# Threshold attention followed by a token and channel mixer: merged transfers, later planned places for VectorE behind transfers, and all of x turned by block transposes

## The chip, the cores and the metric

The kernel runs on one core of one Trainium2 chip. The metric is device time in microseconds (us), lower is better: the median of several runs. The engines are TensorE (PE in the profile, with its weight loads as PEld), VectorE (DVE), ScalarE (ACT), GpSimd (POOL) and SyncE (SP), which here only issues transfers (DMA). Each engine runs its instructions in program order.

## The reference

Eight batches b, eight heads, sequence S = 576, head size 64. Attention keeps only scores within tau of the row's maximum; its output is then x of a mixer block of width 512.

```python
scores = scale * np.matmul(q, k.transpose(0, 1, 3, 2))
thresh = np.max(scores, axis=-1, keepdims=True) - tau
scores = np.where(scores >= thresh, scores, -1000000000.0)
scores = scores - np.max(scores, axis=-1, keepdims=True)
attn = np.exp(scores)
attn = attn / (np.sum(attn, axis=-1, keepdims=True) + 1e-09)
attn_out = np.matmul(attn, v)
x = attn_out.transpose(0, 2, 1, 3).reshape(B, S, H * D)
xt = x.transpose(0, 2, 1)
h = np.maximum(xt @ w_tok1, 0.0) @ w_tok2
u = x + h.transpose(0, 2, 1)
h2 = np.maximum(u @ w_ch1, 0.0) @ w_ch2
return u + h2
```

All arrays are float32 (weights arrive as 64-bit words and are converted in the kernel).

## The kernel before

**Attention.** Heads are taken in pairs (four pairs per batch), and two pairs make a quad of 9 units of 128 query rows, so a batch has 18 units. A round is two units: scores on PE (L825) into the one pair of score tiles, row maxima on DVE (`mx`, L842), the bias on POOL (L848), the mask on ACT (L858), the exponentials on ACT (L868), the inverse sums on DVE (L276, L277), the scaling on POOL (L285). From batch 1 on, the scaled unit `e` is turned in 32x32 blocks on DVE (`turn_blocks`, L315, into a tile `T`), and four transfers per unit (`move`, L327) bring the blocks to the right partitions of `eT`. Three units make a group; a group's values (V: L365 and L370) give a part of x, already transposed, as `xT` (copied by ACT or DVE at L374). So a batch has two quads of three groups. Batch 0 turns `e` on PE (L300) instead.

**Token mixing.** Its first layer needs x with tokens on the partitions, in `x_sb`. In batch 0, PE transposes turn all of x (L435, copied out at L439). From batch 1 on, the first quad's half is turned early, while the second quad is still in attention (`early_x`): two DVE block transposes into the tile `extra` (L395), four transfers to `x_sb` (L406), one small DVE transpose (L401) and four small transfers (L412). The second quad's half is turned by ten PE transposes (L435) after its last V. Then come the first layer on PE (L454), relu, the second layer (L472) and the addition to `xT` on DVE (L483), which makes u.

**Channel mixing.** Groups of 256 rows of u: first layer L948, relu on ACT or DVE (L953, L956), second layer L964. Batch 0 does two such groups at once, batches 1 to 6 one each. For batches from 1 on, u itself is turned back by DVE (L933, into `us`) and transfers (L940, from `us` to `ut`), added to the second layer's result by DVE (L978, into `us`), and stored (L988). `us` has one buffer, so the next L933 waits for these stores. All the rest of u is spilled (L531) and done at the end, from about 904 us on, by another scheme (lines above 1200), which the change leaves alone.

**What sets the order.** The program is written by a planner (class `Scheduler`, L568 on): each operation has an engine, a cost, dependences and a rank (lower goes first); the planner simulates the engines' clocks and eight transfers in flight, and writes each engine's instructions in the order in which it would start them. A dependence on a transfer counts from its planned landing. The score rounds of the next batch are held back by a plan (`planned_at`) so that some channel work of the batch before is left when a batch's attention ends (the planner's constants KEEP and KEEP_LAST, 14 and 20). All transfers in the middle go through SP's one queue, where an instruction that waits holds back all behind it.

**Conversion.** Thirty-one pieces of weights are loaded (L200) into three raw buffers in turn and converted by ACT, DVE and POOL (L239, the last step); the third raw buffer is the place of the last two weight pieces themselves, so the last but one piece has a buffer `spare_a` of its own.

Of the kernel before, what the change touches and what calls it, by code (L numbers as in the profile page):

```python
# [21 lines left out]
def kernel(  # L22
# [166 lines left out]
    def load_piece(i):  # L189
# [7 lines left out]
        if i == len(pieces) - 2:  # L197
            raw_at[i % NRAW] = att.tile([P, 2 * WMAX], U32, tag="spare", bufs=1, name="spare_a")
        raw = raw_at[i % NRAW][0:rows, 0 : n * (2 if wide(i) else 1)].bitcast(src.dtype)
# [110 lines left out]
    def turn_blocks(u):  # L310

        b, p0, t = units[u]
        e = st.pop(u)
        T = Ts[u] = att.tile([P, 4, NK * 32], F32, tag="T", bufs=3, name=f"T_{u}")
        nc.vector.transpose(  # L315
            out=T.rearrange("p a (c x) -> p c a x", c=NK), in_=e.rearrange("p (c a x) -> p c a x", c=NK, a=4)
        )

    def move(u):
        b, p0, t = units[u]  # L320
        key, place = (b, p0, t // GU), t % GU
        if place == 0:
            turned_e[key] = att.tile([P, GU, 4, NK * 32], F32, tag="eT", name=f"eT_{u}")
            eTs[key] = turned_e[key].rearrange("p n i (c x) -> p (n i) c x", c=NK)
        T = Ts.pop(u)
        for i in range(4):
            nc.sync.dma_start(  # L327
                out=turned_e[key][:, place, i, :], in_=T[32 * i : 32 * i + 32]
            )
# [56 lines left out]
    HQ = NP // 2  # L386

    def early_x(b):
# [5 lines left out]
        def turn_main(c):  # L394
            nc.vector.transpose(  # L395
                out=main[:, :, :, c, :].rearrange("q a t d -> q t a d"),
                in_=xT[:, c, 0:MAIN].rearrange("q (t r a) -> q t a r", t=NI, a=4),
            )

        def turn_rest():  # L400
            nc.vector.transpose(  # L401
                out=rest.rearrange("q a c d -> q c a d"), in_=xT[:, 0:HQ, MAIN:S].rearrange("q c (r a) -> q c a r", a=2)
            )

        def move_main(i):
            nc.sync.dma_start(  # L406
                out=x_sb[:, 0:NI, 32 * HQ * i : 32 * HQ * i + 32 * HQ],
# [3 lines left out]
        def move_rest(i):  # L411
            nc.sync.dma_start(  # L412
                out=x_sb[0:LAST, NI, 32 * HQ * i : 32 * HQ * i + 32 * HQ],
# [5 lines left out]
    def token_mlp(b, ps=range(NP)):  # L419
# [4 lines left out]
        turned = ps[HQ:] if b else ps  # L424
# [18 lines left out]
        def tok1(bank, m):  # L443
            if b not in hidden:
                hidden[b] = work.tile([P, NTK, DM], F32, tag="a", bufs=1, name=f"a_{b}")
            if K == L:
                products = [(cols, lambda t: x_sb[:, t, cols])]
            else:
# [37 lines left out]
        for t, n in [(t, n) for t in range(0, NI, n)] + [(NI, 1)]:  # L486
# [62 lines left out]
    FLIGHT, RATE, LANDING = 8, 214.0, 1.5  # L549
# [18 lines left out]
    class Scheduler:  # L568
# [35 lines left out]
        def start(self, x, eng):  # L604
            t = max([d.landed or d.end + (d.lag if d.eng != eng else 0.0) for d in x.deps] + [0.0])
# [113 lines left out]
    CONV = len(pieces)  # L719
    CR = (1, 1, 2)  # L720
# [26 lines left out]
    def make_conversion():  # L747
        for part in range(2):
            put_ac(0, part)
        for i in range(CONV):  # L750
# [5 lines left out]
            put_load(i + NRAW, (key_op("pool", i),))  # L756
# [18 lines left out]
    def make_pair(n):  # L775
# [32 lines left out]
        put(("split", n), sched.op("dve" if n >= NP else "pool", 0.25 if n >= NP else 0.5, lambda: split_middle(n), (key_op("loadv", n), free), 2))  # L808
# [97 lines left out]
    def make_early(b):  # L906

        turn_main, turn_rest, move_main, move_rest = early_x(b)
        have = [key_op("X", rank_of_group(b, 0, g)) for g in range(3)]
        free = early.get(b - 1, converted)  # L910
        turns = [sched.op("dve", 1.1, lambda c=c: turn_main(c), have + free, 2) for c in range(HQ)]
        before = [x for k, x in keyed.items() if k[0] == "tok" and k[1] == b - 1 and len(k) == 3 and x.first_layer]
        moved = [sched.op("sp", 1.2, lambda i=i: move_main(i), turns + before, 0, dmas=(1, 131, 0.645)) for i in range(4)]
        last = sched.op("dve", 0.35, turn_rest, moved, 2)
        moved += [sched.op("sp", 0.6, lambda i=i: move_rest(i), [last] + before, 0, dmas=(1, 16, 0.6)) for i in range(4)]
        early[b] = moved
        xreads.setdefault(b, []).extend(turns + [last])

    def make_groups(b, halves):
        uT = xTs[b]  # L920
        reads = []
        for i in range(NOW[b]):
# [3 lines left out]
            def new_us(s=s, i=i):  # L926
                s["us"] = work.tile([P, nt, 4, NCC * 32], F32, tag="us", bufs=1, name=f"us_{b}_{i}")

            def turn_u(s=s, i=i):
                new_us(s)  # L930
                s["ut"] = work.tile([P, nt, 4, NCC * 32], F32, tag="ut", bufs=1, name=f"ut_{b}_{i}")
                for m in range(nt):
                    nc.vector.transpose(  # L933
                        out=s["us"][:, m].rearrange("q a (c d) -> q c a d", c=NCC),
# [3 lines left out]
            def move_u(k, s=s):  # L938
                for m in range(nt):
                    nc.sync.dma_start(  # L940
# [547 lines left out]
```

## Time and profile before

| what | value |
|---|---|
| time, median of 3 runs | 1267.58 us (1266.56 to 1271.94) |
| the profiled execution: time | 1273.39 us |
| the profiled execution: span of its instructions | 1271.4 us |
| mean granted clock of TensorE | 0.991 |
| 504 transfers eT<-T (L327), 144 KB each | 3.0 us from issue to landing |
| 28 transfers x_sb<-extra (L406), 128 KB each | 3.2 us |
| 28 transfers x_sb<-extra (L412), 16 KB each | 1.9 us |
| 128 transfers ut<-us, 64 KB each | 2.1 us |
| 126 block transposes T<-e on DVE (L315) | 1362 ns each, 170.0 us |
| 14 block transposes extra<-xT on DVE (L395) | 1112 ns each, 15.3 us |
| 12 block transposes us<-xT on DVE (L933) | 1088 ns each, 12.6 us |
| 90 transposes of x on PE (L435) | 10.9 + 3.5 us busy |

The span runs from the first instruction's start to the last one's end. Busy times of an engine can be added up and set against the span; where two instructions of PE overlap in its pipeline, the sum of their own times is more than the room that they take. The granted clock is the share of full speed that TensorE was given. A wait is idle time of an engine, put down to the instruction that released it last.

### The profile page before, as it was taken

The page shows a single profiled execution, that of the slowest core. Times are in us where ns is not written, and L with a number is a line of the kernel's source. Part 1 is how long each engine was busy: PE and PEld are TensorE (multiplying, and loading weights), DVE is VectorE, ACT ScalarE, POOL GpSimd, SP SyncE. Part 2 cuts the span into 40 slices and gives each one's busy share as a digit, 9 for nine tenths or more (in the row PEclk, how much of TensorE's full clock was granted, in tenths as well). Part 3 has the DMA queues.
Part 4 walks back from the last instruction along what each step waited for, and adds up shares of the span by engine and source line. Part 5 has one row for each costly group of instructions (what it writes and reads, how often), then busy time and mean ns, then how long its engine had stood idle before and what let it go on. Part 6 is the DMA issues. An engine that isn't in the chain of part 4 may idle for free.

```text
span 1271.4 us, 21773 instructions
## 1 busy us (share of the span) xinstructions
PE 1237.8 (97%) x8150; PEld 1015.3 (80%) x8150; DVE 755.0 (59%) x1163; ACT 564.0 (44%) x1233; POOL 315.4 (25%) x518
## 2 busy tenths in 40 slices
PE   8888999999999999999989999999999999999998
PEld 7656778797678778878867777888988888888887
DVE  6699982656666667756666756761443534444443
ACT  6998862554645545556465455531110202011120
POOL 4565641232223333323323322410001010000100
PEclk9899999999999999999999999999999999999999
DMA  9546985366777786786776875750212101021011
GB/s 167 139 124 166 214 212 131 87 128 160 168 164 175 160 169 150 165 178 137 179 148 135 187 159 111 179 150 1 60 23 67 34 25 42 18 67 25 26 34 33
DMA packets 324216, 149.23 MB, mean 117 GB/s; under 512 B 223696, under 2 KB 316880, under 8 KB 324112
## 3 DMA queue, kind: packets, MB, share of 16 engines
q1 hardware_dynamic: 322240, 147.64, 50.5%
q8 instruction: 64, 1.05, 0.4%
q10 hardware_dynamic: 1872, 0.21, 0.1%
q14 instruction: 40, 0.33, 0.1%
HBM read 47.32 MB, written 13.50 MB: 48 GB/s over the span
## 4 chain that ended last, share of the span: by engine, by line
PE 78%; SPq 6%; DVE 5%; DMA 5%; ACT 4%; issue 2%; POOL 0%; DVEq 0%; ACTq 0%; POOLq 0%
PE bank L964 11%; PE bank L948 10%; PE o L1309 10%; PE sc L825 9%; PE bank L370 7%; PE hx L1309 6%; PE bank L454 5%; PE hmm L1309 4%; PE oz L1309 4%; PE hz L1309 4%; PE bank L472 4%; SPq L327 3%; PE bank L365 2%; DVE mx L842 2%; ACT e L858 2%
## 5 line engine op out<-in xcount | busy, mean ns | idle before, releaser
L285 POOL TENSOR_SCALAR e<-e,rr 128x576 f32<-128x576 f32 x288 | 213.2, 758 | 299.1 <-DVE rr L277 286.6
L858 ACT ACTIVATE e<-sc,bias 128x576 f32<-128x576 f32 x288 | 194.1, 740 | 156.8 <-POOL bias L848 155.1
L842 DVE TENSOR_REDUCE mx<-sc 128x2 f32<-128x1152 f32 x144 | 188.1, 1347 | 58.9 <-PE sc L825 58.4
L868 ACT ACTIVATE e<-e,ntau 128x576 f32<-128x576 f32 x288 | 220.4, 778 | 0.3
L315 DVE STREAM_TRANSPOSE T<-e 128x1152 f32<-128x1152 f32 x126 | 170.0, 1362 | 36.1 <-POOL e L285 22.2
L948 PE MATMUL bank<-xT,wc 128*128 128x256 f32 x768 | 181.0, 389 | 6.1 <-ACT g L953 5.1
L964 PEld LDWEIGHTS bank<-wc,g 128*128 128x128 f32 x1536 | 178.0, 192 | 10.4 <-issue 2.4
L964 PE MATMUL bank<-wc,g 128*128 128x128 f32 x1536 | 181.4, 276 | 0.9 <-DVE xT L483 0.4
L948 PEld LDWEIGHTS bank<-xT,wc 128*128 128x128 f32 x768 | 144.2, 192 | 36.6 <-ACT g L953 6.5
L825 PE MATMUL sc<-kT,qT 64*128 64x192 f32 (+1 forms) x1920 | 168.8, 337 | 2.7 <-ACT e L858 2.7
L825 PEld LDWEIGHTS sc<-kT,qT 64*128 64x128 f32 (+1 forms) x1920 | 140.8, 179 | 32.1 <-issue 16.3
L370 PE MATMUL bank<-eT,lv 128*64 128x384 f32 (+1 forms) x1024 | 135.2, 406 | 0.0
L1392 POOL TENSOR_TENSOR us<-us,ut 128x256 f32<-128x256 f32 x27 | 22.4, 843 | 391.8 <-DVE us L1230 391.8
L370 PEld LDWEIGHTS bank<-eT,lv 128*64 128x64 f32 x1024 | 74.4, 137 | 49.7 <-issue 41.3
L848 POOL TENSOR_SCALAR bias<-mx,toff 128x2 f32<-128x2 f32 x144 | 38.8, 270 | 197.9 <-DVE mx L842 193.3
L454 PE MATMUL bank<-x_sb,w 128*128 128x256 f32 x320 | 72.8, 383 | 0.3 <-DVE eT L305 0.2
L472 PE MATMUL bank<-w,a 128*128 128x192 f32 (+1 forms) x256 | 72.8, 418 | 0.2 <-DVE xT L483 0.2
L454 PEld LDWEIGHTS bank<-x_sb,w 128*128 128x128 f32 x320 | 59.8, 190 | 11.3 <-issue 1.3
L953 ACT ACTIVATE g<-bank 128x256 f32<-128x256 f32 x66 | 25.3, 383 | 92.9 <-PE bank L948 92.7
L1357 ACT ACTIVATE ga<-hmm 128x256 f32<-128x256 f32 x30 | 11.5, 384 | 116.8 <-PE hmm L1309 116.8
L1230 DVE TENSOR_TENSOR temps<-hx,temps 128x256 f32<-128x256 f32 x60 | 25.1, 418 | 56.7 <-PE hx L1309 56.6
L868 ACT ACTIVATION_READ_ACCUMULATOR e<-e,ntau 128x1 f32 x288 | 58.4, 203 | 0.0
(133 smaller groups left out, 1519.6 us busy)
## 6 DMA issues: line engine op xcount, KB each, us to landing
eT<-T SPq DMA_DIRECT2D x504, 144.0 KB, 3.0
lk<-in_k_dram SPq DMA_DIRECT2D x126, 72.0 KB, 2.9
lq<-in_q_dram SPq DMA_DIRECT2D x124, 72.0 KB, 3.1
out_dram<-us SPq DMA_DIRECT2D x32, 256.0 KB, 2.1
ut<-us SPq DMA_DIRECT2D x128, 64.0 KB, 2.1
lv<-in_v_dram SPq DMA_DIRECT2D x112, 72.0 KB, 2.6
spare<-in_moe_w_ch_dram SPq DMA_DIRECT2D x8, 512.0 KB, 3.9
extra<-in_moe_w_ch_dram SPq DMA_DIRECT2D x8, 512.0 KB, 3.8
```

Of the source, the lines that this page charges most:

```text
L285: nc.gpsimd.tensor_scalar(out=eh, in0=eh, scalar1=rr[:, h : h + 1], scalar2=1.0, op0=ALU.mult, op1=ALU.mult)
L315: nc.vector.transpose(out=T.rearrange("p a (c x) -> p c a x", c=NK), in_=e.rearrange("p (c a x) -> p c a x", c=NK, a=4))
L370: nc.tensor.matmul(to[r], lhsT=lv[:, j, :], rhs=e[j], start=False, stop=(c == NI - 1), skip_group_check=True)
L454: nc.tensor.matmul(to, lhsT=w1[:, t, P * m : P * m + P], rhs=x(t), start=(t == 0), stop=(t == NT - 1), skip_group_check=len(products) > 1,)
L472: nc.tensor.matmul(bank[:, n * i : n * i + n], lhsT=hidden[b][:, m, P * c : P * c + P], rhs=w2[:, m, lo : lo + n], start=(m == 0), stop=(m ...
L825: nc.tensor.matmul(sc[h][rows, f, HT * k : HT * k + HT], lhsT=qT[r, cols], rhs=kT[r, HT * f : HT * f + HT], start=True, stop=True, skip_gr ...
L842: nc.vector.tensor_reduce(out=mx[:, h], in_=sc[h][:, :, 0 : 2 * HT].rearrange("p f (k x) -> p k f x", k=2), axis=AX.XY, op=ALU.max)
L858: nc.scalar.activation(out=eh, in_=part[h], func=AF.Prelu, bias=bias[:, h], scale=SCALE, alpha=STEEP)
L868: nc.scalar.activation(out=eh, in_=eh, func=AF.Exp, bias=ntau, accum_out=rs[:, h, 0:1])
L948: nc.tensor.matmul(bank[:, 0:n], lhsT=wc1[:, j, c, :], rhs=uT[:, c, GR * i : GR * i + n], start=(c == 0), stop=(c == NCC - 1))
L964: nc.tensor.matmul(to, lhsT=s["g"][:, j, P * t : P * t + P], rhs=wc2[:, j, P * c : P * c + P], start=(j == 0 and b > 0), stop=(j == NJ - 1 ...
L1309: nc.tensor.matmul(ps, lhsT=l, rhs=r, start=start and x == 0, stop=x == len(pairs) - 1, skip_group_check=not start)
```

## The change

1. `T` becomes a tile for two units (two buffers instead of three single ones), and `move` takes both units of a round in four transfers when they belong to the same group (six rounds of nine in a batch); otherwise it moves one unit at a time, as before.
2. `us` is laid out by column block first, so that the four moves `ut<-us` carry both 128-row tiles at once (four transfers instead of eight), and the stores read `us` in pieces of 128 columns.
3. `early_x` takes the quad's first pair `c0`; with `EARLY_ALL` the second quad's half of x goes the same way as the first, with rank -1 for its transfers, and the PE transposes of x are left to batch 0 alone. The first layer reads both halves in the block order.
4. The planner counts 2 us (`LATE`) more from a transfer's landing for operations of DVE once PE's planned clock is over 200 us (`CALM`), and has some new costs.
5. The last two conversion pieces use raw buffers 0 and 1; `spare_a` goes, and each of the two is loaded after the conversion of one piece more.

```diff
-        if i == len(pieces) - 2:
-            raw_at[i % NRAW] = att.tile([P, 2 * WMAX], U32, tag="spare", bufs=1, name="spare_a")
-        raw = raw_at[i % NRAW][0:rows, 0 : n * (2 if wide(i) else 1)].bitcast(src.dtype)
+        raw = raw_at[(i + (i >= len(pieces) - 2)) % NRAW][0:rows, 0 : n * (2 if wide(i) else 1)].bitcast(src.dtype)
...
-        T = Ts[u] = att.tile([P, 4, NK * 32], F32, tag="T", bufs=3, name=f"T_{u}")
+        if u % 2 == 0 or u - 1 not in Ts:
+            Ts[u - u % 2] = att.tile([P, 4, 2, NK * 32], F32, tag="T", bufs=2, name=f"T_{u}")
...
         for i in range(4):
-            nc.sync.dma_start(
-                out=turned_e[key][:, place, i, :], in_=T[32 * i : 32 * i + 32]
-            )
+            if len(us) == 2:
+                out, rows = turned_e[key][:, place : place + 2, i, :], T[32 * i : 32 * i + 32]
+            else:
+                out, rows = turned_e[key][:, place, i, :], T[32 * i : 32 * i + 32, :, us[0] % 2, :]
+            nc.sync.dma_start(out=out, in_=rows)
...
-                in_=xT[:, c, 0:MAIN].rearrange("q (t r a) -> q t a r", t=NI, a=4),
+                in_=xT[:, c0 + c, 0:MAIN].rearrange("q (t r a) -> q t a r", t=NI, a=4),
...
-        turned = ps[HQ:] if b else ps
+        turned = ps[HQ:] if b and not EARLY_ALL else ps
...
-            if K == L:
+            if not b:
                 products = [(cols, lambda t: x_sb[:, t, cols])]
+            elif EARLY_ALL:
+                blocks = lambda t, c0: x_sb[:, t, P * c0 : P * c0 + P * HQ].rearrange("p (i c d) -> p c i d", i=4, c=HQ)
+                products = [(slice(P * c0, P * c0 + P * HQ), lambda t, c0=c0: blocks(t, c0)) for c0 in (0, HQ)]
...
-        for t, n in [(t, n) for t in range(0, NI, n)] + [(NI, 1)]:
+        for t, n in [(t, n) for t in range(0, NI, n) if not b or not EARLY_ALL] + [(NI, 1)] * (not b or not EARLY_ALL):
...
-    FLIGHT, RATE, LANDING = 8, 214.0, 1.5
+    FLIGHT, RATE, LANDING, LATE, CALM = 8, 214.0, 1.5, 2.0, 200.0
...
-            t = max([d.landed or d.end + (d.lag if d.eng != eng else 0.0) for d in x.deps] + [0.0])
+            late = LATE if eng == "dve" and self.clock["pe"] > CALM else 0.0
+            t = max([d.landed + late if d.landed else d.end + (d.lag if d.eng != eng else 0.0) for d in x.deps] + [0.0])
...
-            put_load(i + NRAW, (key_op("pool", i),))
+            if i + NRAW < CONV - 2:
+                put_load(i + NRAW, (key_op("pool", i),))
+            elif i + NRAW - 1 >= CONV - 2:
+                put_load(i + NRAW - 1, (key_op("pool", i),))
...
-    def make_early(b):
+    def make_early(b, c0=0):
...
-        have = [key_op("X", rank_of_group(b, 0, g)) for g in range(3)]
-        free = early.get(b - 1, converted)
-        turns = [sched.op("dve", 1.1, lambda c=c: turn_main(c), have + free, 2) for c in range(HQ)]
+        have = [key_op("X", rank_of_group(b, c0, g)) for g in range(3)]
+        free = early.get(b if c0 else b - 1, converted)
+        turns = [sched.op("dve", 1.02, lambda c=c: turn_main(c), have + free, 2) for c in range(HQ)]
...
-        moved = [sched.op("sp", 1.2, lambda i=i: move_main(i), turns + before, 0, dmas=(1, 131, 0.645)) for i in range(4)]
+        rank = -1 if c0 else 0
+        moved = [sched.op("sp", 1.2, lambda i=i: move_main(i), turns + before, rank, dmas=(1, 131, 0.67)) for i in range(4)]
...
-                s["us"] = work.tile([P, nt, 4, NCC * 32], F32, tag="us", bufs=1, name=f"us_{b}_{i}")
+                s["us"] = work.tile([P, 4, nt, NCC * 32], F32, tag="us", bufs=1, name=f"us_{b}_{i}")
...
-                for m in range(nt):
-                    nc.sync.dma_start(
-                        out=s["ut"][:, m, k, :], in_=s["us"][32 * k : 32 * k + 32, m]
-                    )
+                nc.sync.dma_start(out=s["ut"][:, :, k, :], in_=s["us"][32 * k : 32 * k + 32])
...
-                nc.sync.dma_start(out=out[b, t0 : t0 + P, :], in_=s["us"][:, t].rearrange("q a x -> q (a x)"))
+                nc.sync.dma_start(out=out[b, t0 : t0 + P, :].rearrange("q (c x) -> q c x", c=NCC), in_=s["us"][:, :, t, :])
...
-                turn = sched.op("dve", 1.2, turn_u, have + state["stores"] + state["adds"] + (converted if b == 1 else []), 5)
+                turn = sched.op("dve", 2.05, turn_u, have + state["stores"] + state["adds"] + (converted if b == 1 else []), 5)
...
-                moved = [sched.op("sp", 1.2, lambda k=k, m=move_u: m(k), (turn,), 1, dmas=(nt, 53, 0.645)) for k in range(4)]
+                moved = [sched.op("sp", 1.2, lambda k=k, m=move_u: m(k), (turn,), 1, dmas=(1, 107, 0.67)) for k in range(4)]
...
-                stores.append(sched.op("sp", 0.35, lambda t=t, f=store: f(t), outs, 2, dmas=(1, 150, 0.35)))
+                stores.append(sched.op("sp", 0.35, lambda t=t, f=store: f(t), outs, 2, dmas=(1, 270, 0.55)))
...
-            deps += [key_op("T", u - 1), key_op("M", u - 3)]
-            put(("T", u), sched.op("dve", 1.31, lambda u=u: turn_blocks(u), deps, 4))
...
+            v = u - u % 2
+            deps += [key_op("T", u - 1), key_op("M", v - 4), key_op("M", v - 3)]
+            put(("T", u), sched.op("dve", 1.3, lambda u=u: turn_blocks(u), deps, 4))
...
+        same = units[us[0]][0:2] == units[us[1]][0:2] and units[us[0]][2] // GU == units[us[1]][2] // GU
+        for moved in [us] if same else [us[0:1], us[1:2]]:
...
+                [key_op("T", u) for u in moved] + [key_op("V", G - 2) if t % GU == 0 else None],
...
+                dmas=(4, 147 * len(moved), 0.67),
...
+                    if p0 == NP - 2 and EARLY_ALL:
+                        late_due.append(b)
...
+        while late_due and key_op("V", rank_of_group(late_due[0], NP // 2, 2)).end is not None:
+            make_early(late_due.pop(0), NP // 2)
```

## The prediction

> **What bounds the kernel now.** I read the page's engine totals first, then who TensorE (PE) waited for, then the timeline at those waits and at the places where the changed instructions sit, last the busy time of each engine by stretches of one batch.
>
> ```profile
> PE 1237.8 (97%) x8150; PEld 1015.3 (80%) x8150; DVE 755.0 (59%) x1163; ACT 564.0 (44%) x1233; POOL 315.4 (25%) x518
> ...
> PE 78%; SPq 6%; DVE 5%; DMA 5%; ACT 4%; issue 2%; POOL 0%; DVEq 0%; ACTq 0%; POOLq 0%
> ...
> PE bank L948 <- ACT g L953: 5.1, 3, 2.6
> ...
> PE bank L365 <- DMA x_sb<-extra: 1.9, 1, 1.9
> ...
> PE bank L435 <- ACT x_sb L439: 1.0, 2, 0.7
> PE bank L365 <- DMA lv<-in_v_dram: 1.0, 2, 0.6
> ```
>
> PE is busy 97% of 1271.4 us and carries 78% of the chain that ended last. It idles 33.6 us in all; some 15 us of that lie before 128 us (32.00 less the 28.13, 27.91, 28.34 and 28.52 us of the first four stretches of 32 us), where the order hardly changes (the first T is at 115.5), and 4.5 us lie in the last stretch, mostly after the last matmul. So a PE instruction taken out of the middle is worth its own spacing, and only PE's few waits there can be won besides. The wait lines give who waited, for what, us in total, times and the longest.
>
> ```profile
> 645.00:750.00 105.00, 102.28 (x762) 80.84 (x760) 69.35 (x102) 55.31 (x121) 30.82 (x54) 0.98 0.71 157
> ```
>
> This is one batch: length, then busy PE, weight loads, DVE, ACT and POOL, granted clock, DMA share. DVE has a third of the time free, DMA engines 29%.
>
> **The transposes that go.** For batches 1 to 7 the second half of x is turned by PE, ten transposes a batch (eight of 128 rows, two of 64) at L435: 70 of the 90 in the profile. Batch 7:
>
> ```profile
> 852.00 1.99 PE L948 MATMUL bank<-xT,wc 128*128 128x256 f32 x8
> 853.84 0.60 PE L435 MATMUL bank<-ident,xT 128*128 128x128 f32 x4
> 854.27 1.89 PE L948 MATMUL bank<-xT,wc 128*128 128x256 f32 x8
> 856.00 0.60 PE L435 MATMUL bank<-ident,xT 128*128 128x128 f32 x4
> 856.44 1.89 PE L948 MATMUL bank<-xT,wc 128*128 128x256 f32 x8
> 858.17 0.38 PE L435 MATMUL bank<-ident,xT 128*64 128x128 f32 x2
> 858.39 3.62 PE L948 MATMUL bank<-xT,wc 128*128 128x256 f32 x16
> ```
>
> Busy times overlap, so I count from start to start. From 852.00 to 858.39 are 6.39 us for 24 matmuls and 10 transposes; eight such matmuls alone take 1.73 us (872.20 to 873.93), so the ten cost 6.39 - 5.19 = 1.20. Batch 3, where they stand between other work, gives 0.49 + 0.55 + 0.31 = 1.35. I take 1.25 x 7 = **-8.7**. Summed busy time (70 of about 0.16) would say 11.2, but that counts overlap. PE also waited 0.97 us for the copies of these banks (0.74 at 346.93, 0.23 at 556.31): **-1.0**. The copies themselves, two of 0.585 and one of about 0.36 us per batch on ACT or DVE, lie off PE's path: 0.
>
> **What replaces them.** Per batch two transposes of 128x512 on DVE (L395, 1.10 each), one of 128x128 (L401, 0.31), and eight transfers on SP (L406 0.63 and L412 0.60 us of issue each): 17.6 us of DVE in all, 5 us of SP per batch. DVE's free 35 us per batch cover it: 0 on the path, and where that cover fails it is the third rival. The latency counts more. After the last values (V) of a batch come 2 x 1.10 for the turns, three issues of 0.65 and 3.2 to land, 0.31, then three issues of 0.62 and 1.9 to land: 11.5 us at least. Each step can stand behind a reduce pair of 2.6 on DVE (L842) or eight moves of 5.1 on SP, so 15 to 18 is my estimate. Until now the first token matmul (L454) came 4.0 us after the last V's copy in batch 2 (343.37 to 347.41), 12.6 in batch 3 and 9.2 in batch 7. PE's cover is the previous batch's second channel layer: at 343 us all eight of its blocks (L964, 2.68 each, 21.4 us) are still to come, at 852 us seven L948 blocks and eight of L964. Spending the cover there leaves less between the token steps, whose banks wait for DVE. Bounds: 0, and one wait like the 1.88 at 339.41 in each batch, 13. I take 0.5 a batch, since the planner sees the latency and may pull scores forward: **+3.5**.
>
> **Merged transfers.** Six of nine pairs of units per batch share a group, so T moves go from 72 to 48 issues a batch, u's from 8 to 4; x adds 8. That frees 24 x 0.60 + 4 x 0.60 - 5 = 12 us of SP per batch. I take issue time as independent of size: the 16 KB transfers at L412 take 0.60, the 144 KB moves at L327 also 0.60; the other bound, issue doubling with size, makes the merge worth 0. A merged move of 288 KB lands later than the 3.0 us of one by at most its bytes at the busiest slice's 214 GB/s, 0.7 us, and its first unit waits for the second's transpose (1.37); both lie inside the spare latency of a round. Output rows of batches 0 to 6 in the first pass now leave in runs of 512 B instead of 2 KB: stores land in 2.1 us before; the nearest row with short runs is x_sb, 3.2 for half the bytes. What waits for a store is DVE's next L933, that is the following point.
>
> **Later places behind transfers.** Two events show the price of a DVE instruction queued too early; the first:
>
> ```profile
> 631.60 0.59 SPq L988 DMA_DIRECT2D out_dram<-us  x1
> ...
> 634.41 2.08 DVE L933 STREAM_TRANSPOSE us<-xT 128x512 f32<-128x512 f32 x2 [3.95 <-DMA out_dram<-us]
> ...
> 637.68 2.58 DVE L842 TENSOR_REDUCE mx<-sc 128x2 f32<-128x1152 f32 x2
> ...
> 639.39 1.37 ACT L858 ACTIVATE e<-sc,bias 128x576 f32<-128x576 f32 x2 [3.94 <-POOL bias L848]
> ...
> 641.09 3.55 PE L948 MATMUL bank<-xT,wc 128*128 128x256 f32 x8 [2.60 <-ACT g L953]
> ```
>
> The store stood behind fifteen SP issues (from 619.55 on), DVE stood behind the store, the reduce behind DVE, ACT's mask behind the reduce and ACT's copy of a bank behind that mask. PE waited 2.60 us and its next eight matmuls took 3.55 instead of 1.99. At 746.38 the same: 2.08, then 3.54. Together 2.60 + 1.56 + 2.08 + 1.55 = 7.8. With LATE the planner counts 2 us more before DVE work that follows a transfer, and SP's queue is shorter by up to half of its moves, 4 x 0.60. Bounds 0 and 7.8; I take **-5**, as 3.95 of DVE's wait exceeds what either repair alone gives (2, 2.4) but not both. The other waits for transfers in the middle (1.88, 0.63, 0.35) are 2.9. They are V's waits for T moves and v loads, whose queue gets shorter, but the late x moves with rank -1 now go ahead of them: **-1** of bounds 0 and -2.9.
>
> The granted clock in those 4 us was 0.61. The Trainium skill ("TensorE: Matmul & The Clock Gate", section "Part 1: The HAM clock gate") gives half rate only after an idle window of about 3.4 us; here 2.60 and even 2.08 us of idle were followed by half speed. By the page the term would lose 3.1 of its 7.8 and the sum would come out 2 us higher; the trace decides.
>
> **Conversion.** The last two weight pieces lose their own buffer and each loads one GpSimd step (2.5 us, 160.09 to 162.59) later; the second channel layer of batch 0 begins at 175.02, while the last conversion ends at 176.04. Bounds 0 and 2.5 plus a half-clock spell of 1.6; merged moves let that load go out sooner (it stood behind twelve T moves of 8.5 us): **+1**.
>
> **Sum.** 1271.4 - 8.7 - 1.0 + 3.5 - 5 - 1 + 1 = 1260.2 of span, and with 2.0 around it (1273.39 - 1271.4) 1262.2 for an execution like the profiled one. That one was 5.8 above the median, so the change of -11.2 is set against 1267.58: **1256.4 us**. If the median runs lack the two events, the time is 1261.
>
> **Rivals.**
> 1. All waits go and nothing new comes: 1267.6 - 8.7 - 1.0 - 7.8 - 2.9 = 1247. For it: every stall in the middle is one of the planner's misjudged transfers. Against: each new order brought its own.
> 2. The stalls only move (the new order makes other DVE instructions wait) and the latency costs 1 us a batch: 1267.6 - 9.7 + 7 = 1265. For it: the L365 wait at 339.41 stands behind x moves, of which there are now twice as many.
> 3. DVE becomes the bound at the end of a batch, and its added 17.6 us stand on the path: 1267.6 - 9.7 + 17.6 = 1275.5. Against: 66% busy. The Trainium skill ("VectorE: DVE Perf Modes", section "Rules for kernel authors") would keep full 128x128 transposes on TensorE when PSUM will do as destination; that speaks for this rival.
> 4. Slower: the chain V, turn, move, turn, move outlasts PE's cover. It decides from 21.4 us of L964 plus two score rounds of 2.15, about 26. Batch 5's early chain, which nothing hurried, ran from 606.67 to 631.5 plus 1.9, 27 us. Then PE waits about 2.6 a batch and runs 1.56 longer at half clock; in six batches (the last has more cover) 25 us: 1267.6 - 9.7 + 25 = 1283. Against: the late moves have rank -1, ahead of T moves; early ones had 0.
>
> **How the numbers follow.** Forecast 0.58, rival 1 0.15, rival 2 0.11, rival 3 0.04, rival 4 0.12. Half a per cent, 6.3 us, is what a measurement of this kernel can tell from no change: faster means below 1261.2. The forecast's own range is 1251 to 1262; a twentieth of it falls above 1261.2. So faster is 0.55 + 0.15 = 0.70, same 0.03 + 0.11 = 0.14, slower 0.04 + 0.12 = 0.16. The range takes in rivals 1 and 2: 1247 to 1268; rivals 3 and 4 stay outside.
>
> **What would show it.** L435 at 20 transposes, L395 at 28 and L401 at 14; T moves at 336; PE busy lower by 8 to 11 us. No L933 or L842 behind an output store for 4 us, no granted clock below 0.98 in a batch's stretch after 224 us. Wrong if L454 is released by x_sb transfers for over 1 us per batch, if L472 waits for DVE's L483 in every batch, or if PE's idle time after 224 us grows.

## The result and the profile after

The time went up where the prediction said down: **1282.69 us** (median of 6 runs, 1279.24 to 1290.16) against 1266.53 for the kernel before beside it (6 runs), ratio 1.0124, 95% interval 1.0092 to 1.0157. The forecast was 1256.4. The profiled execution of the changed kernel took 1279.24 us, its span 1277.5; it was the fastest of its six runs, and the one of the kernel before (1273.39) was slower than all of its six, so the two profiles lie only 6 us apart. First its page: the engine totals, the shares of the chain that ended last, and the transfers that changed (KB each, median us from issue to landing).

```profile
PE 1229.3 (96%) x8080; PEld 1009.5 (79%) x8080; DVE 765.3 (60%) x1171; ACT 560.0 (44%) x1225; POOL 315.3 (25%) x518
...
PE 72%; SPq 10%; DVE 8%; DMA 5%; ACT 2%; issue 2%; POOL 0%; DVEq 0%; ACTq 0%; POOLq 0%
...
eT<-T SPq DMA_DIRECT2D x168, 288.0 KB, 5.4
eT<-T SPq DMA_DIRECT2D x168, 144.0 KB, 3.1
```

PE has 8.5 us less to do and the span is 6.1 us longer, so PE's idle time rose from 33.6 to 48.2 us. The chain shows where: its share of PE fell from 78% to 72%, and SP's queue and DVE took it. PE's waits name the releasers (us in total, times, the longest):

```profile
PE bank L367 <- DMA lv<-in_v_dram: 9.2, 2, 7.5
PE bank L367 <- DMA eT<-T: 9.0, 3, 3.8
```

Both are V (L365 before, L367 now) waiting for its inputs. The old waits of L948 for `g` (5.1 us, most of them behind an output store) are gone. The same view by stretches (columns as in the prediction) puts most of the new waits into two places, the end of the conversion and batch 2:

```profile
160.00:192.00 32.00, 24.46 (x176) 17.54 (x175) 25.10 (x38) 17.02 (x38) 14.54 (x20) 0.89 0.88 201
329.00:434.00 105.00, 95.84 (x703) 74.70 (x702) 66.68 (x98) 49.97 (x107) 28.65 (x51) 0.95 0.79 163
645.00:750.00 105.00, 102.90 (x772) 82.31 (x769) 73.19 (x101) 57.39 (x125) 33.37 (x59) 1.00 0.81 171
```

Before, PE was busy all 32.00 us of the first stretch at full clock, and 100.61 of the second. The third, the batch shown in the prediction, is as good as it was (102.28), with DMA at 81% instead of 71%. Of the stretches not shown, 750 to 855 us lost 3.2 us and 434 to 540 lost 2.0, while 540 to 645 gained 2.2. After 224 us PE's idle time rose from 17.0 to 24.1 us, which the prediction had named as a sign of being wrong.

### The profile page after: what moved, and what is told of

It is laid out like the page before. It is cut to its first block, busy times and chain, and to the rows that moved or that the text cites. A ratio compares the mean times of both kernels' runs of the same rounds, so it can differ in the third digit from the quotient of the medians.

```text
span 1277.5 us, 21370 instructions
## 1 busy us (share of the span) xinstructions
PE 1229.3 (96%) x8080; PEld 1009.5 (79%) x8080; DVE 765.3 (60%) x1171; ACT 560.0 (44%) x1225; POOL 315.3 (25%) x518
## 4 chain that ended last, share of the span: by engine, by line
PE 72%; SPq 10%; DVE 8%; DMA 5%; ACT 2%; issue 2%; POOL 0%; DVEq 0%; ACTq 0%; POOLq 0%
PE bank L973 11%; PE o L1329 10%; PE bank L957 10%; PE sc L836 8%; PE hx L1329 6%; PE bank L372 6%; SPq L331 5%; PE hmm L1329 4%; PE oz L1329 4%; PE hz L1329 4%; PE bank L460 4%; SPq L106 3%; DVE mx L853 2%; PE bank L478 2%; PE bank L367 2%; DVE T L314 2%
## 5 line engine op out<-in xcount | busy, mean ns | idle before, releaser
L957 PE MATMUL bank<-xT,wc 128*128 128x256 f32 x768 | 175.4, 384 | 0.8 <-DVE xT L489 0.8
L372 PE MATMUL bank<-eT,lv 128*64 128x384 f32 (+1 forms) x1024 | 138.5, 413 | 0.0
L367 PE MATMUL bank<-eT,vl 128*64 128x384 f32 (+1 forms) x256 | 45.9, 437 | 21.5 <-DMA lv<-in_v_dram 9.2
L478 PEld LDWEIGHTS bank<-w,a 128*128 128x128 f32 x256 | 43.3, 190 | 25.3 <-issue 5.8
```

Source lines behind the costliest of these rows:

```text
L372: nc.tensor.matmul(to[r], lhsT=lv[:, j, :], rhs=e[j], start=False, stop=(c == NI - 1), skip_group_check=True)
L478: nc.tensor.matmul(bank[:, n * i : n * i + n], lhsT=hidden[b][:, m, P * c : P * c + P], rhs=w2[:, m, lo : lo + n], start=(m == 0), stop=(m ...
L957: nc.tensor.matmul(bank[:, 0:n], lhsT=wc1[:, j, c, :], rhs=uT[:, c, GR * i : GR * i + n], start=(c == 0), stop=(c == NCC - 1))
```

## The experiments

Each expectation names its theories itself. Eighteen kernels, made from the kernel after by putting parts back, so that parts can be counted one at a time. Each ratio is to the kernel before on the same chip, with its 95% interval; kernels of different groups ran on different chips, so they are compared by ratios (0.1% is 1.27 us). "Mended" is the kernel after with the conversion's own buffer back.

**One part undone at a time**

```diff
# no_merge
-            Ts[u - u % 2] = att.tile([P, 4, 2, NK * 32], F32, tag="T", bufs=2, name=f"T_{u}")
+        Ts[u] = att.tile([P, 4, NK * 32], F32, tag="T", bufs=3, name=f"T_{u}")
...
-                s["us"] = work.tile([P, 4, nt, NCC * 32], F32, tag="us", bufs=1, name=f"us_{b}_{i}")
+                s["us"] = work.tile([P, nt, 4, NCC * 32], F32, tag="us", bufs=1, name=f"us_{b}_{i}")
# pe_turns_x
-    EARLY_ALL = True
+    EARLY_ALL = False
# no_late
-    FLIGHT, RATE, LANDING, LATE, CALM = 8, 214.0, 1.5, 2.0, 200.0
+    FLIGHT, RATE, LANDING, LATE, CALM = 8, 214.0, 1.5, 0.0, 200.0
# neither: all three
```

> The changed kernel with both merges undone (T moves one unit at a time from three single tiles, u moved in eight transfers and stored in 2 KB runs); all of x still by block transposes, LATE 2, conversion as changed. Theory A (merging is at fault: a 288 KB move lands in 5.4 us where 144 KB took 3.0, and SP is held 1.03 us per issue instead of 0.71): the V waits of 9 us go, SP's time for T moves stays near 350 us, and the time is 1255 to 1266. Theory B (turning the second half of x by blocks is at fault: 56 more transfers in the middle and the first token layer 18 to 36 us later in a batch): 1278 to 1290, since SP gets still more issues. Theory C (LATE is at fault): 1278 to 1285.

Measured: 1283.75 us, ratio 1.0102 (1.0073 to 1.0131). Nothing that can be told from the kernel after: theory A fell.

> The changed kernel with EARLY_ALL off: the second quad's half of x goes back to ten PE transposes a batch; merges, LATE and conversion as changed. Theory A: PE gets 8.7 us of transposes back and the merged moves stay, 1285 to 1292. Theory B: the late x moves leave SP's queue and the first token layer comes 4 to 13 us after the last V's copy again, 1262 to 1270. Theory C: 1282 to 1292.

Measured: 1290.45 us, 1.0157 (1.0128 to 1.0186): 0.33% over the kernel after by the ratios, though the intervals overlap. Theory B fell; in this company the block transposes are at least no loss.

> The changed kernel with LATE set to 0: the planner counts DVE's work from a transfer's planned landing, as before the change; merges and x as changed. Theory A and theory B: DVE's work behind transfers comes too early again, and the landing of merged moves is late by 2.4 us, so 1282 to 1295. Theory C (planning DVE later delays the scores and V, and nothing else is at fault): 1256 to 1268.

Measured: 1294.22 us, 1.0190 (1.0158 to 1.0222): the later places are a gain of 0.66%, some 8 us, and theory C fell. Taken out one at a time, none of these three parts was at fault.

> The changed kernel with merges, block transposes of the second half and LATE all off: of the change only the later loads of the last two conversion pieces and the planner's new costs are left. If these are harmless, within 4 us of the kernel before (1262 to 1271). If the conversion's 7.5 us wait of PE at 182 us is their doing, that wait is still there and the time is 1272 to 1280.

Measured: 1279.92 us, 1.0084 (1.0051 to 1.0118). With none of the three parts left, only the conversion and the planner's costs differ from the kernel before, and most of the loss is still there. In the stretch of 160 to 192 us PE is busy 27.52 us of 32. That pointed to the conversion.

**The conversion.** The timeline of the kernel after around the conversion's end shows what happened (start, us, engine, line, operation, what it writes and reads, count; in brackets the idle time before it and its releaser):

```profile
156.39 8.54 SPq L331 DMA_DIRECT2D eT<-T  x8
...
159.59 1.36 POOL L237 TENSOR_TENSOR wc<-wc,extra 128x512 int32<-128x512 int32 x1 [1.99 <-DVE wc L229]
...
165.04 0.53 SPq L198 DMA_DIRECT2D extra<-in_moe_w_ch_dram  x1
...
169.06 0.53 SPq L198 DMA_DIRECT2D spare<-in_moe_w_ch_dram  x1
...
181.79 1.30 POOL L237 TENSOR_TENSOR wc<-wc,spare 128x512 int32<-128x512 int32 x1 [2.56 <-ACT e L869]
182.34 1.55 PE L367 MATMUL bank<-eT,vl 128*64 128x384 f32 x4 [7.54 <-DMA lv<-in_v_dram]
```

And the same place in the kernel before:

```profile
153.76 1.30 POOL L239 TENSOR_TENSOR wc<-wc 128x512 int32<-128x512 int32 x1 [1.20 <-issue]
...
155.74 0.86 SPq L200 DMA_DIRECT2D spare_a<-in_moe_w_ch_dram  x1
156.71 8.51 SPq L327 DMA_DIRECT2D eT<-T  x12
...
165.64 0.35 SPq L200 DMA_DIRECT2D extra<-in_moe_w_ch_dram  x1
...
174.75 1.29 POOL L239 TENSOR_TENSOR wc<-wc,extra 128x512 int32<-128x512 int32 x1 [3.67 <-ACT e L868]
```

Before, the load of the last but one piece had to wait for the POOL step that ended at 155.06; it went out at 155.74, just ahead of the T moves. Now it waits for one POOL step more, which ends at 160.95, 5.9 us later. By then it has missed its place and stands behind 8.54 us of moves, so that it goes out at 165.04, 9.3 us later than before; the last piece follows at 169.06 instead of 165.64, and the last conversion starts at 181.79 instead of 174.75. Batch 0's second channel layer, which filled PE from 175.02 on, starts at 187.08. PE is bare for 7.54 us, and its next four matmuls take 1.55 us instead of the usual 0.87.

Two kernels test it. One puts the buffer back (in the pool of the token layer's hidden tile, which has room) and the other is the kernel before with the new costs alone; two more look at what is left.

```diff
# conv_mended
-        raw = raw_at[(i + (i >= len(pieces) - 2)) % NRAW][0:rows, 0 : n * (2 if wide(i) else 1)].bitcast(src.dtype)
+        if i == len(pieces) - 2:
+            raw_at[i % NRAW] = work.tile([P, 2 * WMAX], U32, tag="a", bufs=1, name="spare_a")
+        raw = raw_at[i % NRAW][0:rows, 0 : n * (2 if wide(i) else 1)].bitcast(src.dtype)
...
-            if i + NRAW < CONV - 2:
-                put_load(i + NRAW, (key_op("pool", i),))
-            elif i + NRAW - 1 >= CONV - 2:
-                put_load(i + NRAW - 1, (key_op("pool", i),))
+            put_load(i + NRAW, (key_op("pool", i),))
# conv_mended_no_merge: no_merge, and the conversion as in the kernel before
# conv_mended_late_pe: conv_mended and
-            late = LATE if eng == "dve" and self.clock["pe"] > CALM else 0.0
+            late = LATE if eng in ("dve", "pe") and self.clock["pe"] > CALM else 0.0
```

> The kernel before with the planner's new costs alone (1.3 for T, 2.05 for u's turn, 0.67 of issue and the like); no merge, no late x, LATE 0, conversion as before. Theory D (the later loads of the last two conversion pieces cost 8 to 9 us: batch 0's second channel layer starts 7 to 12 us later and PE waits at 177 to 182 us): 1266 to 1271, no PE wait over 1 us between 160 and 192 us. Theory E (any new order brings stalls of its own, and the costs alone do it): 1275 to 1282, with the stalls elsewhere than at 180 us.

Measured: 1271.46 us, 1.0013 (0.9997 to 1.0028): the costs alone do not change the time. They do change the order: the two waits of DVE of 4 us behind output stores are not in its profile (one of 1.78 is left), and PE has another instead, 3.98 us before L971, where DVE stands 3.81 us behind a load of V.

> The changed kernel with the conversion's loads as before the change: the last but one piece goes to a raw buffer of its own again, which borrows the place of the token layer's hidden tile (tag a, idle between batch 0 and batch 1). Merges, late x, LATE as changed. Theory D: PE's wait of 7.5 us at 182 us and the half clock behind it go, 1271 to 1276. Theory E: within 4 us of the changed kernel, 1279 to 1287.

Measured: 1275.35 us, 1.0043 (1.0022 to 1.0065).

```profile
160.00:192.00 32.00, 32.00 (x253) 25.67 (x254) 24.38 (x37) 18.96 (x44) 15.03 (x20) 1.00 0.84 181
```

In this stretch of the mended kernel PE is busy throughout again. Mending takes 0.81% off the kernel after; between `neither` and `costs_only`, where nothing else differs, it is 0.71%.

> No merges (T and u as before the change), conversion as before with spare_a; block transposes for all of x and LATE 2 as changed. Theory D: 1283.75 less 8 to 9, 1274 to 1277; the V waits at 344 and 363 us of the run without merges (2.8 and 3.0, with half clock) remain. If in addition those waits came from the conversion's delay: 1258 to 1265. Theory E: 1280 to 1288.

Measured: 1276.66 us, 1.0059 (1.0037 to 1.0081): 0.43% under `no_merge`, which has the conversion's delay besides. A fourth pair, `pe_turns_x` and `merged_late_places` below, gives 0.68%. So the conversion costs 0.4 to 0.8%, 5 to 10 us.

> conv_mended, and LATE counts for PE's operations behind transfers too (V behind T moves, the first token layer behind x moves). If V's waits are misjudged landings (5.4 us measured for a merged move, 2.9 planned), they shrink from 9 us to under 3 and the time falls 4 to 8 us below conv_mended's, 1264 to 1270. If they are latency that nothing covers, PE waits as long at other places: within 3 us of conv_mended.

Measured: 1273.67 us, 1.0027 (1.0007 to 1.0046), not told from the mended kernel; V's waits for T moves fell from 8.8 to 5.6 us, and other waits came.

**Each part added alone.** The mended kernel is still slower than the one before, though PE has 8.7 us less to do. So the parts were put onto the kernel of costs alone, one by one (single moves; the conversion as before).

```diff
# late_x_only: costs_only and
-    EARLY_ALL = False
+    EARLY_ALL = True
# late_places_only: costs_only and
-    FLIGHT, RATE, LANDING, LATE, CALM = 8, 214.0, 1.5, 0.0, 200.0
+    FLIGHT, RATE, LANDING, LATE, CALM = 8, 214.0, 1.5, 2.0, 200.0
```

> The kernel before with the planner's new costs and, of the change, only the second half of x turned by block transposes: single moves, LATE 0, the conversion's loads as before (no part of the computation left out). Theory F: the new x chain takes some 19 us from the last V to the first token matmul where the transposes on PE took 4 to 13, the planner fills that time with the next batch's rounds, and those run later with no channel work beside them, so that V's waits for T moves and the scores' waits for ACT show. Then this alone, without the 2 us of LATE, is slower than the kernel of costs only (1271.5): 1276 to 1288, with waits of 2 to 4 us before V or scores between 330 and 540 us. Rival G: the chain is covered and what the mended kernel lost came from LATE: then PE's 8.7 us are won here, 1261 to 1265.

Measured: 1280.38 us, 1.0100 (1.0078 to 1.0122): 0.87% over the costs alone, with PE's transposes gone. PE after the last V of batch 2, in its timeline:

```profile
330.94 1.99 PE L955 MATMUL bank<-xT,wc 128*128 128x256 f32 x8
...
334.80 2.78 PE L370 MATMUL bank<-eT,lv 128*64 128x384 f32 x16
337.51 2.38 PE L831 MATMUL sc<-kT,qT 64*64 64x192 f32 x36
343.25 0.59 PE L831 MATMUL sc<-kT,qT 64*128 64x192 f32 x2 [3.35 <-ACT e L864]
344.51 3.70 PE L831 MATMUL sc<-kT,qT 64*128 64x192 f32 x22 [0.67 <-ACT e L864]
352.42 1.55 PE L365 MATMUL bank<-eT,vl 128*64 128x384 f32 x4 [4.21 <-DMA eT<-T]
353.72 4.79 PE L370 MATMUL bank<-eT,lv 128*64 128x384 f32 x16
358.44 8.90 PE L458 MATMUL bank<-x_sb,w 128*128 128x256 f32 x40
```

The last V (334.80) ends at 337.6 and the first token matmul (L458) starts at 358.44, 20.8 us later; with x turned on PE it is 4 to 13. The last block of channel work (L955) starts at 330.94. What PE has in between is the next batch's score rounds, one after the other, each waiting for the mask of the round before it (3.35 and 0.67 us), and a V that waits 4.21 us for T moves; half speed follows. Batch 3 shows the same at 457.86 and 466.75 (4.37 and 3.42 us). The chain is long in itself, some 14 us without any wait, and it stood three times behind other work, twice in SP's queue:

```profile
336.00 2.63 SPq L120 DMA_DIRECT2D lv<-in_v_dram  x4
338.74 2.79 SPq L329 DMA_DIRECT2D eT<-T  x4
341.62 2.85 SPq L407 DMA_DIRECT2D x_sb<-extra  x4
344.57 2.70 SPq L120 DMA_DIRECT2D lv<-in_v_dram  x4
347.37 5.11 SPq L329 DMA_DIRECT2D eT<-T  x8
352.58 3.71 SPq L413 DMA_DIRECT2D x_sb<-extra  x4
```

The x moves (L407), ready when the two turns end at 340.19, go out 1.4 us later, behind V's loads and T moves. They have landed at 346.86, but DVE's last turn ends only at 351.15, behind block transposes and row maxima of the next round: 4.0 us. The small moves (L413) then stand 1.4 us behind the eight T moves of a round.

> The kernel before with the planner's new costs and LATE of 2 us, nothing else (no part of the computation left out). Theory F: with x's second half turned on PE the order keeps its cover; LATE takes away waits of DVE behind stores or moves that the kernel of costs only has (4.0 us before L971 behind DVE, 5 us of others), so 1262 to 1269. Rival G: LATE is what moves rounds away from their cover, and waits of 2 to 4 us before V appear between 330 and 540 us: 1273 to 1280.

Measured: 1262.93 us, 0.9958 (0.9944 to 0.9972): faster than both kernels. LATE is worth 0.55% here, as theory F had it; the wait of 3.98 us before L971 is gone. A third pair, `conv_mended_no_merge` against `late_x_only`, gives 0.41%.

**Where the channel work is kept.** If cover is what lacks at a batch's end, keeping more of it there should help.

```diff
# keep_22, keep_30: conv_mended and (22.0, 22.0), (30.0, 30.0)
-    KEEP, KEEP_LAST = 14.0, 20.0
+    KEEP, KEEP_LAST = 22.0, 22.0
```

> The kernel after with the conversion's own buffer back, and KEEP 22 instead of 14 (KEEP_LAST 22 instead of 20): the next batch's rounds are planned 8 us earlier, so more channel work is left when a batch's attention ends (no part of the computation left out). Theory F: the waits before V and scores in batches 2 and 3 shrink by half or more, the granted clock of 329 to 434 us comes back from 0.95 to 0.98 or more: 1265 to 1271 against the 1275.4 of KEEP 14. Rival H: the moves of T are late by themselves (DMA share 0.79, SP's queue full), whatever stands beside them: 1273 to 1279.

Measured: 1282.49 us, 1.0122 (1.0100 to 1.0143).

> As the run with KEEP 22, with KEEP and KEEP_LAST 30. Theory F: no less than with 22, 1262 to 1270, if there are enough score rounds to be pulled forward. Rival H: 1273 to 1279. A third way: the rounds are pulled forward as soon as score tiles are free, so that KEEP no longer binds: the same as with 22 within 2 us.

Measured: 1288.10 us, 1.0153 (1.0138 to 1.0168). Both misses, and all the theories fell. With KEEP 22 V waits 10.1 us in all for T moves, 8.8 with KEEP 14, and 10.0 behind `us` on DVE instead of 0.7.

**Work or latency, and merging with x on PE.** `late_x_dead` has the whole new chain run into a tile that nothing reads, while the token layer takes PE's transposes as before.

```diff
# late_x_dead: late_places_only, the buffer of conv_mended, and
+    x_dead = const.tile([P, NI, P * NP // 2], F32, name="x_dead")
...
-                out=x_sb[:, 0:NI, P * c0 + 32 * HQ * i : P * c0 + 32 * HQ * i + 32 * HQ],
+                out=(x_dead if c0 else x_sb)[:, 0:NI, 32 * HQ * i : 32 * HQ * i + 32 * HQ],
...
-        early[b] = early.get(b, []) + moved
+        (dead if c0 else early)[b] = moved
# merged_late_places: conv_mended and EARLY_ALL = False
# late_places_pe: late_places_only and LATE for "pe" as well
# keep_6, keep_minus_2: conv_mended and KEEP 6.0, -2.0
# late_places_pe_keep_6: late_places_pe and KEEP 6.0
```

> The kernel with LATE and the new costs alone (1262.9), and in each batch from 1 on the whole chain of the second half of x besides (two turns of 128x512 and one of 128x128 on DVE, eight transfers on SP with rank -1), whose blocks go to a tile that nothing reads; PE's ten transposes of x stay and the token layer waits for them alone. So it has all the new work of DVE, SP and the DMA engines and none of the latency. Theory L (latency: PE runs out of channel work before x has arrived): 1261 to 1267, the first token matmul 4 to 13 us after the last V as before. Rival W (the work on DVE and SP delays reduces and moves): 1270 to 1285.

Measured: 1274.18 us, 1.0036 (1.0019 to 1.0053): 0.78% over `late_places_only` (10 us, +-3). This was the rival's side: the work on DVE and SP alone, with no matmul waiting for its result, costs as much as the transposes on PE that it replaces. In the profiles, PE's span of 1273.3 us instead of 1259.9 is 7.4 us of longer busy time (1235.9 for 1228.5) and 6 us more idle. Most of it stands at three waits of V in batches 2, 4 and 6, for x moves, for ACT and for T moves, and at the half speed behind them:

```profile
336.85 1.55 PE L366 MATMUL bank<-eT,vl 128*64 128x384 f32 x4 [2.96 <-DMA x_sb<-extra]
338.16 5.12 PE L371 MATMUL bank<-eT,lv 128*64 128x384 f32 x16
...
551.12 1.55 PE L366 MATMUL bank<-eT,vl 128*64 128x384 f32 x4 [3.21 <-ACT e L875]
552.43 3.81 PE L371 MATMUL bank<-eT,lv 128*64 128x384 f32 x16
...
771.64 0.87 PE L366 MATMUL bank<-eT,vl 128*64 128x384 f32 x4 [2.60 <-DMA eT<-T]
772.31 4.47 PE L371 MATMUL bank<-eT,lv 128*64 128x384 f32 x16
```

At full speed the pairs take 0.87 and 2.78 us, so the three spells cost 6.4 us of busy time. `late_places_only` has the first of these waits too, but full speed after it:

```profile
335.91 0.87 PE L365 MATMUL bank<-eT,vl 128*64 128x384 f32 x4 [3.24 <-DMA x_sb<-extra]
336.57 2.78 PE L370 MATMUL bank<-eT,lv 128*64 128x384 f32 x16
```

So by these rows 3 us of the difference between the two profiles are the chance of the clock, not work of the chain.

> The kernel after with the conversion's own buffer back and the second half of x turned on PE: merged transfers and LATE alone. Theory M0 (merging is neutral, as with all of x in blocks, and the slowness of the run with x turned on PE is the conversion's): 1261 to 1267, as LATE alone. Rival M1 (a merged move lands 2.4 us later and its first unit waits for the second's turn, which costs where the token layer follows the last V at once): 1272 to 1284, with waits for eT<-T before V.

Measured: 1281.73 us, 1.0089 (1.0060 to 1.0117): 1.31% over the same kernel with single moves. So merging is not neutral; it was so only beside the late chain of x. Its waits:

```profile
PE bank L369 <- DMA eT<-T: 7.9, 3, 3.4
...
PE bank L369 <- DMA lv<-in_v_dram: 4.1, 3, 2.6
PE bank L369 <- DMA lk<-in_k_dram: 2.4, 1, 2.4
```

In the kernel with single moves, `late_places_only`, V waits for no T move at all:

```profile
PE bank L365 <- DMA lv<-in_v_dram: 3.6, 2, 2.3
PE bank L365 <- DMA x_sb<-extra: 3.2, 1, 3.2
```

> The kernel after with the conversion's own buffer back, and KEEP 6 instead of 14 (KEEP_LAST stays at 20): less channel work is left at a batch's end, more of it lies between the rounds. If cover is one sum that is shared by the rounds and the batch's end, and KEEP 22 lost because the rounds lacked it: 1270 to 1280, either less at the rounds or more at the end. If KEEP 14 lies at the best place: 1277 to 1290.

Measured: 1271.04 us, 1.0010 (0.9992 to 1.0027), 0.33% under KEEP 14: the first of the two, cover as one sum, and the least of the series.

> The kernel with LATE and the new costs alone (1262.9), LATE counted for PE's operations as well as DVE's: V of a unit is planned 2 us later behind the T moves. Where this took 1.7 us off the mended kernel, 1259 to 1263 here; if V's waits there came from the late x chain alone, 1262 to 1266.

Measured: 1260.38 us, 0.9926 (0.9904 to 0.9948), the best kernel of the study, 0.7% below before; against `late_places_only` the intervals just touch.

> The kernel after with the conversion's own buffer back, and KEEP -2 (KEEP_LAST stays at 20): the series so far is 1288.1, 1282.5, 1275.4, 1271.0 for 30, 22, 14, 6, some 0.7 us for each us of KEEP. Theory R (the rounds lack cover: a round's chain from scores to eT is longer with merged moves, so channel work belongs between the rounds, not at the batch's end): 1263 to 1269. Rival E: at the batch's end nothing is left to cover the chain of x, of some 20 us, and the series turns: 1272 to 1285.

Measured: 1298.59 us, 1.0226 (1.0199 to 1.0254). The series turns, and further than rival E had it. With 30, 22, 14, 6 and -2 the ratios are 1.0153, 1.0122, 1.0043, 1.0010 and 1.0226; at -2 the waits are those of `late_x_only`, at the batch's end:

```profile
PE sc L835 <- ACT e L868: 11.7, 11, 3.2
...
PE bank L369 <- DMA x_sb<-extra: 5.5, 1, 5.5
```

> The kernel with single moves, x's second half turned on PE, LATE for DVE and PE and the new costs (1260.4), with KEEP 6 instead of 14. Theory R, that the lack at the rounds comes from the longer chains of the change: here 14 suits, 1259 to 1264. Rival: less KEEP is better in any of these orders: 1252 to 1258.

Measured: 1264.93 us, 0.9950 (0.9933 to 0.9968). In the order without the change's longer chains, 6 is no better than 14: the rival fell, and theory R's range was missed by 1 us.

**The parts in a row.** By ratios, from the kernel before: costs +0.13%, LATE -0.55, late x +1.01, merging -0.16, conversion +0.81: together 1.24%. These prices hold in that sequence, and the -0.16 cannot be told from zero. Merging costs 1.31% where x is turned on PE, and after it late x is worth -0.46% (-0.33%, not told from zero, between the kernel after and `pe_turns_x`). So the two do not add up. My reading is that both draw on the same spare time of a round, and whichever comes first pays for it; no run measures that spare time.

## Why the prediction was wrong

The forecast's sum was -11.2 us; the change gave +16.2. Two steps failed, and they make up the difference between them: turning the second half of x in blocks, which I had at -6.2 us (transposes and their copies off PE, 0 for the work, +3.5 for the latency) and which in the row of parts above is +1.01%, 12.8 us; and the conversion, which I had at +1 and which is +0.81% there, 10 us.

- **Transposes off PE, -8.7.** Right: 20 of 90 are left and PE's busy time fell by 8.5, half-speed spells included.
- **What replaces them, 0 on the path.** The first step that failed. "DVE's free 35 us per batch cover it" counted free time as an average. `late_x_dead` puts the price of that work at 10 us, at three waits of V and the half speed behind them (3 us of it the clock's chance). The Trainium skill ("VectorE: DVE Perf Modes", section "Rules for kernel authors") would keep full 128x128 transposes on TensorE; these runs agree where moves are single (blocks cost 0.87% and 1.01%), and not beside merged moves (-0.46%).
- **Latency of the late x, +3.5.** Mis-sized. I took 0.5 a batch "since the planner sees the latency and may pull scores forward". It did pull them forward, and these rounds in a row are what stood bare. From `late_x_dead` to `conv_mended_no_merge` it is +0.23%, 2.9 us, while 9.7 us of PE's work and waits go: 12.6, close to my upper bound of 13 (worked out, if the two add; the intervals leave it open by 3.5 either way). The chain took 20.8 us in batch 2 where I had estimated 15 to 18. Rival 4 had this mechanism; its 1283 met the measured time by luck: 5 to 10 us of that time were the conversion's.
- **Merged transfers, 0 on the path.** The mechanism was wrong in both numbers. I took issue time as independent of size. In SP's timeline of before, eight T moves of 144 KB,

```profile
557.81 5.14 SPq L327 DMA_DIRECT2D eT<-T  x8
```

  and in that of the kernel after, four merged ones of 288 KB:

```profile
587.38 4.85 SPq L331 DMA_DIRECT2D eT<-T  x4
```

  On average 1.21 us each instead of 0.64, so in the sum the bound "issue doubling with size" was near, and SP gained nothing: its T moves took 315.6 us of issue before and 317.0 after. But the first two of four merged moves in a row take 0.63 us (median), like single ones; the third and fourth take 1.74 and 1.78, and a small load soon behind them is held too:

```profile
586.09 0.49 SPq L106 DMA_DIRECT2D lk<-in_k_dram  x1
...
592.98 1.45 SPq L106 DMA_DIRECT2D lk<-in_k_dram  x1
```

  What is under way ahead of a transfer holds the queue; what limits it is not shown. And a merged move lands after 5.4 us, 2.4 later than 3.0, not 0.7. The price on the path was -0.16% here, 1.31% without the late x. I let the spare latency of a round pay for it, while the late x, as I read it, drew on the same.
- **Later places, -5.** The size was near: -0.55% (7 us) alone, -0.66% in the kernel after. The kind of mechanism was right, but not the events that I priced, so the size was partly luck: the two waits of 4 us behind stores are gone with the new costs alone, and nothing was gained by that. What LATE took away was another wait of DVE behind a transfer (3.81 us, before L971) and smaller ones.
- **Waits for copies and for V's inputs, -1.0 and -1.** The copies' waits went with the transposes. V's waits for transfers did not shrink: 2.9 us before, 18.2 after, of which 7.5 are the conversion's.
- **Conversion, +1.** The second step that failed: 5 to 10 us over four pairs of kernels, against my bounds of 0 to 4.1. I priced one POOL step of 2.5 us for both loads and counted on merged moves to "let that load go out sooner". The step of 2.5 is the last piece's; the last but one waits for the step before it, and was ready 5.9 us later. It then lost its place in SP's queue as well, to 8.54 us of moves, and went out 9.3 us later. Those eight, merged ones among them, took as long as twelve single ones did before (8.51). PE's wait of 7.54 us came out of that.
- **The range** of 1247 to 1268 left out rivals 3 and 4, to which I gave 0.16. The bounds of the terms, added up, went past 1268: most terms were taken near their kind end.

What stays open: which instruction of the dead chain delays V at those three places, and why merging costs 1.31% beside PE's transposes of x and nothing beside the late chain. Every edit makes the planner write another order, and prices of 2 to 3 us cannot be told from the luck of one order.

## What to carry over

An instruction that is ready later in an in-order queue is late by its own delay and by the block of transfers that now goes ahead of it (5.9 us became 9.3 here); look for that block before pricing the delay. A latency that PE must cover is paid from the work that is left at that moment, and the runs with KEEP suggest that cover is one sum: two edits that each fit into it may not fit together, and work kept for a batch's end is missing between its rounds. Of this change the later places alone, counted for PE as well, are the part to keep (0.9926; 0.9958 with DVE alone).

## What was not expected of the hardware

- A transfer twice as large (288 for 144 KB, between the same tiles) took 1.21 us of SP's queue on average instead of 0.64 and landed in 5.4 us instead of 3.0. It is the third and fourth in a row that are held (1.74 and 1.78 us); the first two take 0.63. Where four merged moves took the place of eight, neither the queue's time nor the latency got shorter.
- Half clock after idle time. In all twenty profiled kernels I took V's first four matmuls (0.87 us at full clock, 1.55 at half) and the sixteen behind them (2.78 us at full clock) after every wait of over 1 us between 130 and 900 us. After waits of 1.06 to 2.06 us, all 42 ran at full clock. After 2.07 to 3.42 us it was 11 of 29, and after 3.70 us and more none of 16. The Trainium skill ("TensorE: Matmul & The Clock Gate", section "Part 1: The HAM clock gate") says that the clock falls after at least one idle window of about 3.4 us; these rows agree from 3.70 us on, but a wait of 2.07 us was enough at times, so about 2 us is the longest wait that never cost clock in these runs.
